# Attention tiles inside the dense blocks: four stages of the second and third tile start one slot later

## The chip, the cores and the metric

One core of a Trainium2 chip runs the whole program. The time is the device time of one execution in microseconds (us). The kernel before takes 1057.63 us in the median of three runs (1057.42 to 1059.7). One more execution was profiled; its rows stand below. TensorE is called PE, its weight loads PEld, VectorE DVE, ScalarE ACT, GpSimd POOL and SyncE SP, as in the profile.

## The reference

The program is three layers one behind the other, all in float32.

```python
# 1. chunked attention: 4 batches, 8 heads, 768 positions, head size 64
for c in range(24):                       # chunks of 32 queries
    k_full = concat([mem_k, k[c*32-16 : c*32+40]])     # 8 memory keys, 16 left, 8 right
    v_full = concat([mem_v, v[c*32-16 : c*32+40]])
    a = softmax(q[c*32 : c*32+32] @ k_full.T / 8)
    out[c*32 : c*32+32] = a @ v_full
x = out as (3072, 512)
# 2. dense layer, 512 -> 2048 -> 512
h = x @ w_in;  x = (h * clip(h + 3, 0, 6) / 6) @ w_out
# 3. eight experts, one for each token, chosen by cosine likeness
logits = normalise(x) @ normalise(expert_emb).T / tau
e = argmax(logits);  gate = softmax(logits)[e]
out = gate * (relu(x @ w1[e]) @ w2[e])
```

## The kernel before

The 3072 tokens are 24 tiles of 128, and the tiles make eight blocks of 4, 2, 3, 3, 3, 3, 3 and 3 (`BS`; `F0` is the first tile of each block). The program goes through the blocks of the dense layer, and while block `bl` is worked on, two other things are laid between its steps: the attention of the three tiles of block `bl + 1`, and the router of block `bl - 1`. Behind the last block comes the expert stage.

A block has 16 steps `f`, one for each 128 of the 2048 inner columns. In a step PE does `mm1(bl, f + 1)` (12 matmuls, L434, into a bank `h`) and later `mm2(bl, f)` (9 matmuls, L488, into three banks `acc`). What is to be laid between stands in dictionaries: `pre_[f]` runs before `mm1(bl, f + 1)`, `slot[f]` between it and `mm2(bl, f)` (L1168 to 1176). A function in a slot issues its instructions on all engines at that place, and every engine works through its own list in this order. ACT and DVE have, behind each `mm1`, the gate of its result: ACT relu (L447), DVE `g` (L448), ACT `gh` (L442), DVE `gl` (L443); `mm2` of the next step needs `gh` and `gl`.

A tile of attention has six stages (`stages(i)`), each in a slot of its own:

- `st_t(i + 1, i)`: keys of the tile after, and queries. From tile 9 on (`VT`, the tenth) DVE transposes the keys (L219) and the queries (L257, tile `qT`), POOL copies the edges of the keys to the neighbouring windows (L223 to 230). Then SP issues the loads of the next keys and queries, 16 small DMAs each (L144).
- `st_s`: 64 small matmuls into the double bank `s` (L275); DVE takes the maximum (L287) and subtracts it (L292, tile `e`), ACT makes exp (L295). In the last tile of a batch DVE sets an edge before that (L285).
- `st_n`: DVE sums and inverts (L308 to 310).
- `st_pt`: four PE transposes of `e` into the bank `att` (L319), ACT copies them out (L321, tile `pT`).
- `st_av`: 64 matmuls into `s` (L333), DVE multiplies (L340, tile `xo`); then SP loads the values of the tile after the next (L178, L188).
- `st_xt`: four PE transposes of `xo` into `att` (L203), ACT makes `xh` (L368), DVE the rest `xl` (L370).

`att` is one PSUM bank. The router uses it too: `r_t` (transposes L525, then a split of four steps in turn on ACT and DVE, L543, L545, L547, L549), `r_l` (12 small matmuls, L558, and a DVE reduction, L561), `r_rank` (L609 to 627) and `r_list` (L649, L650, matmuls with the tiles `sel` that `r_sel` makes on DVE, L639 to 641, three operations for each tile). In blocks with three routed tiles `r_t` stands in slots 1 and 4 and in `pre_[7]`, `r_l` in `pre_[4]`, slot 6 and `pre_[8]`, `r_rank` in slot 9, `r_sel` in slot 10, `r_list` in slot 11, `r_gate` with its three writes to `xb` (SP, L686) in slot 12. The tiles `qT` and `pT` are one buffer, `e` and `xo` another, the bank `s` a third.

The diff touches the numbers that place the stages of blocks 2 to 6. The first tile of a block has slots 0, 1, 2, 3, 4, 5. The second has 4, 5, 6, 7, 9, 10 and the third 9, 10, 11, 12, 14, 15. Stages are put in with `insert(0, ...)`, so in a slot that two tiles share the later tile's stage comes first: in slot 4 `st_t` of the second tile comes ahead of `st_av` of the first, in slot 5 `st_s` of the second ahead of `st_xt` of the first.

Of the kernel before, what the change touches and what calls it, by code (L numbers as in the profile page):

```python
# [30 lines left out]
def attn_moe_kernel(ctx, tc, q, k, v, mem_k, mem_v, w_in, w_out, emb, tau, w1, w2, out, dbg=None):  # L31
# [485 lines left out]
    def r_t(bl, t, pt=None, more=None):  # L517

        if t == 0:
            blk[bl] = (small([P, BS[bl]], name="ss"), small([P, BS[bl], E], name="lg"))  # L520
        x2 = x2_t[bl, t]
        if pt is None:
            pt = bank("att", 1)
        for j in range(KD):
            nc.tensor.transpose(pt[:, j * P:(j + 1) * P], x2[:, j * P:(j + 1) * P], ident)  # L525
        if t == BS[bl] - 1 and more:
            q = [sb.tile([P, DM], BF16, tag=n, name="x2T", bufs=2) for n in ("gh", "gl")]
        else:
            q = sb.tile([P, 2, DM], BF16, tag="dec", name="x2T", bufs=2)
            q = [q[:, i, :] for i in range(2)]  # L530
        mid = late["x2"][2][:, t * DM // 2:(t + 1) * DM // 2] if bl == 0 else x2[:, XW + 1:XW + 1 + DM // 2]
        parts = q[0], mid.bitcast(BF16), q[1]
        x2T[bl, t] = parts
        if more is None:
            split3([(pt, parts)], nc.scalar)
        else:
            more.append((pt, parts))
# [13 lines left out]
    def r_l(bl, t, pl=None):  # L551
        parts = x2T.pop((bl, t))
        own = pl is None
        pl = bank("att", 1) if own else pl[:, 3 * E * t:]
        for j in range(KD):
            for i, xt in enumerate(parts):
                w = (3 - i) * E
                nc.tensor.matmul(pl[:, 0:w], lhsT=xt[:, j * P:(j + 1) * P], rhs=en_t[:, j, 0:3 - i, :].rearrange("p a e -> p (a e)"),  # L558
                                 start=(j == 0 and i == 0), stop=(j == KD - 1 and i == 2))
        if own:  # L560
            V.tensor_reduce(out=blk[bl][1][:, t, :], in_=pl[:, 0:3 * E].rearrange("p (a e) -> p e a", a=3), axis=AX.X, op=ALU.add)  # L561

    def r_ss(bl, t):
        junk = sb.tile([P, DM], F32, tag="dec", name="junk", bufs=2)
        nc.scalar.activation(out=junk, in_=x2_t[bl, t][:, 0:DM], func=AF.Square, accum_out=blk[bl][0][:, t:t + 1])
        if t == BS[bl] - 1:
            blk[bl] = (root(blk[bl][0]),) + blk[bl][1:]
# [16 lines left out]
    def r_route(bl):  # L584

        ss, lg = blk[bl]
        TB = BS[bl]
        sh = [P, TB, E]
        mx = small([P, TB], name="r_mx")
        V.tensor_reduce(out=mx, in_=lg, axis=AX.X, op=ALU.max)  # L590
        eq = small(sh, name="r_eq")
        V.tensor_tensor(out=eq, in0=lg, in1=mx.unsqueeze(2).to_broadcast(sh), op=ALU.is_equal)
        V.tensor_tensor(out=eq, in0=eq, in1=rev.unsqueeze(1).to_broadcast(sh), op=ALU.mult)
        m2 = small([P, TB], name="r_m2")
        V.tensor_reduce(out=m2, in_=eq, axis=AX.X, op=ALU.max)
        oh = small(sh, F16, name="r_oh")
        V.tensor_tensor(out=oh, in0=eq, in1=m2.unsqueeze(2).to_broadcast(sh), op=ALU.is_equal)
        blk[bl] = (ss, lg, oh, mx)
# [46 lines left out]
    def r_list(bl, pT=None, defer=False):  # L645

        pT = (bank("att", 1) if pT is None else pT)[:, 0:NCOL]
        for t, (r0, r1, c) in enumerate(blk[bl][4]):
            nc.tensor.matmul(pT, lhsT=r0, rhs=c, start=(t == 0), stop=False)  # L649
            nc.tensor.matmul(pT, lhsT=r1, rhs=c, start=False, stop=(t == BS[bl] - 1))  # L650

        def add():
            V.tensor_tensor(out=lists, in0=lists, in1=pT, op=ALU.add)

        if defer:
            return add
        add()
# [304 lines left out]
    with tc.manual_schedule():  # L962
# [15 lines left out]
        def stages(i):  # L978
            def a():
                st_t(i + 1 if i + 1 < NT else None, i)  # L980

            def s_():
                st_s(i)

            def p_():
                st_pt(i)

            def v_():
                st_av(i)
                if i + 2 < NT:  # L990
                    load_mv(i + 2)
                    load_v(i + 2)

            def x_():
                st_xt(i)
            return [a, s_, lambda: st_n(i), p_, v_, x_]
# [11 lines left out]
        st = [stages(i) for i in range(BS[0] + BS[1] + 1)]  # L1008
# [95 lines left out]
        def spare(bl):  # L1104

            if bl == NB - 1:
                return bank2()[:, 0, :]
            if bl == 1 and "px" not in late:
                late["px"] = bank("acc", 3)
            return late["px"] if bl == 1 else None  # L1110

        for bl in range(NB):
            slot, pre_ = {}, {}
            if bl == 0:
                continue
            if bl + 1 < NB:
                if bl == 1:
                    slot[0] = [a6[5]]
                for a in range(bl == 1, TB):
                    st = stages(F0[bl + 1] + a)  # L1120
                    for o, f_ in zip((0, 2, 3, 4, 6, 7) if bl == 1 else (0, 1, 2, 3, 4, 5) if a == 0 else (-1, 0, 1, 2, 4, 5), st):
                        slot.setdefault((1, 8)[a - 1] + o if bl == 1 else 5 * a + o, []).insert(0, f_)
            if bl:
                d = 2 if bl == 1 else 0
                for t in range(BS[bl - 1]):
                    (wt, f), (wl, f2) = (RT4 if bl == 1 else RT)[t], (RL4 if bl == 1 else RL)[t]
                    (pre_, slot)[wt].setdefault(f, []).append(lambda t=t: r_t(bl - 1, t, spare(bl)))
                    (pre_, slot)[wl].setdefault(f2, []).insert(0, lambda t=t: r_l(bl - 1, t))
                    slot.setdefault((8, 8, 9, 9)[t] + d // 2, []).append(lambda t=t: r_ss(bl - 1, t))
                slot.setdefault(8 + d, []).append(lambda: r_route(bl - 1))  # L1130
                slot.setdefault(9 + d, []).append(lambda: r_rank(bl - 1))
                slot.setdefault(10 + d, []).append(lambda: r_sel(bl - 1))
                slot.setdefault(11 + d, []).append(lambda: r_list(bl - 1))
                slot.setdefault(12 + d, []).append(lambda: r_exp(bl - 1))
                slot.setdefault(12 + d, []).append(lambda: r_gate(bl - 1))
                if bl == EB + 1:
                    slot.setdefault(12, []).append(pick_first)
                    slot.setdefault(14, []).append(pick_rest)
            if bl == NB - 1:
                at_ctx.close()  # L1140
                p2["pool"] = ctx.enter_context(tc.tile_pool(name="p2", bufs=1, side="right", reuse_waits="tile"))
                for n in range(NE):
                    load_x(("E", n))
                eE = [nc.values_load(e0i[0:1, n:n + 1], engines=[SP], min_val=0, max_val=E - 1) for n in range(2)]
                todo = [(st, p, i) for p in range(4) for st in range(2) for i in range(2)]
                rws = {}

                def pre(n=1):
                    for _ in range(n):
                        if todo:  # L1150
                            st, p, i = todo.pop(0)
                            rws[st, p, i] = load_half(p, i, eE[st])

                def go(st, p, i, eng=None):
                    split_half(st, p, i, rws.pop((st, p, i)), eng)
                    pre()

                pre(RW)
                for n, f in enumerate(SP_):
                    slot.setdefault(f, []).append(lambda n=n: go(n // 2 % 2, n // 4, n % 2, nc.gpsimd if n in PG else None))  # L1160
                slot.setdefault(1, []).append(plan_const)
                slot.setdefault(13, []).append(lambda: T_x(("E", 0)))
            if bl == 1:
                evac(0)
            mm1(bl, 0)
            if bl > 1:
                evac(bl - 1)
            for f in range(KF):  # L1168
                for g_ in pre_.get(f, []):
                    g_()  # L1170
                if f + 1 < KF:
                    mm1(bl, f + 1)
                for g_ in slot.get(f, []):
                    g_()
                if bl < NB - 1 or f < KF - 1:
                    mm2(bl, f)
# [75 lines left out]
        for i in range(2, len(seq)):  # L1252
            n, st = seq[i]
# [70 lines left out]
```

## Time and profile before

| what | value |
|---|---|
| median of three runs | 1057.63 us |
| the profiled execution | 1059.21 us, its span 1057.5 us |
| PE busy | 1006.4 us, 95% of the span |
| DVE, ACT, POOL busy | 529.9, 416.8, 163.6 us |
| blocks 2 to 6 | 218.6 to 630.1 us of the span |
| one of blocks 3 to 6 | 82 us |

The profile counts an engine as idle before an instruction and names what ended the idle time. A step of a block is cut here at the first matmul of `mm1`; such a piece holds `mm1(f + 1)`, slot `f`, `mm2(f)` and `pre_[f + 1]`. Durations are those of the engine's records; neighbouring PE matmuls overlap in them.

### The profile page before, as it was taken

The page shows a single profiled execution, that of the slowest core. Times are in us where ns is not written, and L with a number is a line of the kernel's source. Part 1 is how long each engine was busy: PE and PEld are TensorE (multiplying, and loading weights), DVE is VectorE, ACT ScalarE, POOL GpSimd, SP SyncE. Part 2 cuts the span into 40 slices and gives each one's busy share as a digit, 9 for nine tenths or more (in the row PEclk, how much of TensorE's full clock was granted, in tenths as well). Part 3 has the DMA queues.
Part 4 walks back from the last instruction along what each step waited for, and adds up shares of the span by engine and source line. Part 5 has one row for each costly group of instructions (what it writes and reads, how often), then busy time and mean ns, then how long its engine had stood idle before and what let it go on. Part 6 is the DMA issues. An engine that isn't in the chain of part 4 may idle for free.

```text
span 1057.5 us, 23039 instructions
## 1 busy us (share of the span) xinstructions
PE 1006.4 (95%) x8230; PEld 840.9 (80%) x8230; DVE 529.9 (50%) x1174; ACT 416.8 (39%) x743; POOL 163.6 (15%) x209
## 2 busy tenths in 40 slices
PE   8798999999999999999999999998999999999994
PEld 4576778878888888788888888886888888888783
DVE  5677855544545545545545555755134423326530
ACT  5343444433333333333333334662234523336531
POOL 1133760000000000000000010043112111112210
PEclk9899999999999999999999999999999999999998
DMA  9655531232222222232231122332035514247510
GB/s 193 147 164 174 169 113 37 39 68 32 38 67 31 39 72 31 38 78 32 38 75 29 22 83 103 125 90 71 31 111 157 176 40 148 89 152 241 199 50 22
DMA packets 171837, 95.55 MB, mean 90 GB/s; under 512 B 138709, under 2 KB 146933, under 8 KB 171712
## 3 DMA queue, kind: packets, MB, share of 16 engines
q1 hardware_dynamic: 167104, 80.54, 29.0%
q0 software_dynamic: 4448, 13.42, 4.0%
q8 instruction: 66, 1.08, 0.4%
q14 instruction: 59, 0.48, 0.2%
q10 hardware_dynamic: 160, 0.02, 0.0%
HBM read 156.83 MB, written 13.38 MB: 161 GB/s over the span
## 4 chain that ended last, share of the span: by engine, by line
PE 67%; DVE 12%; issue 7%; ACT 6%; DMA 3%; SPq 2%; POOL 1%; POOLq 0%; DVEq 0%; ACTq 0%
PE acc L488 18%; PE h L434 18%; PE acc L836 11%; PE h L805 11%; PE s L814 2%; PE s L333 1%; DVE g L448 1%; SPq L144 1%; DVE mx L287 1%; ACT g L447 1%; ACT gh L442 1%; DVE e L292 1%; PE att L787 1%; DVE dec L412 1%; PE att L319 1%
## 5 line engine op out<-in xcount | busy, mean ns | idle before, releaser
L488 PE MATMUL acc<-wo,gh 128*128 128x512 f32 x640 | 206.5, 404 | 2.5 <-DVE x L505 1.5
L434 PE MATMUL h<-xh,w_in_h 128*128 128x384 f32 (+2 forms) x512 | 175.7, 343 | 5.6 <-DVE wo L470 2.4
L434 PE MATMUL h<-xl,w_in_h 128*128 128x384 f32 (+2 forms) x512 | 173.1, 338 | 0.1
L434 PE MATMUL h<-xh,w_in_l 128*128 128x384 f32 (+2 forms) x512 | 172.5, 337 | 0.0
L447 ACT ACTIVATE g<-h,three 128x384 f32<-128x384 f32 (+1 forms) x112 | 63.4, 566 | 176.9 <-PE h L434 176.2
L488 PEld LDWEIGHTS acc<-wo,gh 128*128 128x128 f32 x640 | 113.1, 188 | 23.0 <-ACT x L507 2.6
L488 PE MATMUL acc<-wo,gl 128*128 128x512 f32 x320 | 126.2, 394 | 0.0
L448 DVE SCALAR_TENSOR_TENSOR g<-g,h 128x384 f32<-128x384 f32 (+1 forms) x112 | 59.8, 534 | 127.3 <-ACT g L447 126.7
L434 PEld LDWEIGHTS h<-xh,w_in_h 128*128 128x128 f32 x512 | 96.4, 188 | 14.4 <-DVE wo L470 3.9
L434 PEld LDWEIGHTS h<-xl,w_in_h 128*128 128x128 f32 x512 | 96.6, 189 | 7.2 <-DVE xl L370 1.0
L434 PEld LDWEIGHTS h<-xh,w_in_l 128*128 128x128 f32 x512 | 96.4, 188 | 2.9
L443 DVE TENSOR_TENSOR gl<-g,gh 128x384 fp32r<-128x384 f32 (+1 forms) x112 | 60.8, 543 | 63.2 <-ACT gh L442 63.2
L442 ACT CAST gh<-g 128x384 fp32r<-128x384 f32 (+1 forms) x112 | 55.8, 498 | 77.7 <-DVE g L448 77.7
L792 DVE TENSOR_TENSOR tl<-att,th 128x512 fp32r<-128x512 f32 x26 | 18.0, 692 | 113.5 <-ACT th L791 107.6
L488 PEld LDWEIGHTS acc<-wo,gl 128*128 128x128 f32 x320 | 60.1, 188 | 14.2 <-DVE gl L443 0.6
L773 POOL DMA_INDIRECT xg<-xb,m_ix x27 | 27.9, 1032 | 261.9 <-PE h L805 212.2
L223 POOL COPY kt<-kt 128x192 f32<-128x192 f32 x15 | 5.2, 346 | 373.5 <-DVE kt L219 373.5
L836 PE MATMUL acc<-wo,th 128*128 128x512 f32 x192 | 60.6, 397 | 0.0
L791 ACT CAST th<-att 128x512 fp32r<-128x512 f32 x26 | 15.2, 587 | 107.3 <-PE acc L836 105.6
L808 ACT ACTIVATE hs<-h 128x512 f32<-128x512 f32 x54 | 32.1, 597 | 64.3 <-PE h L805 60.4
L836 PE MATMUL acc<-w_in_h,th 128*128 128x512 f32 x120 | 49.0, 408 | 0.0
L805 PE MATMUL h<-wo,th 128*128 128x512 f32 x192 | 48.9, 397 | 0.0
(318 smaller groups left out, 1820.0 us busy)
## 6 DMA issues: line engine op xcount, KB each, us to landing
rw<-in_moe_w_dram SPq DMA_DIRECT2D x136, 512.0 KB
vw<-in_v_dram SPq DMA_DIRECT2D x176, 56.0 KB
raw_in<-in_moe_w_in_dram SPq DMA_DIRECT2D x16, 512.0 KB
raw_out<-in_moe_w_out_dram SPq DMA_DIRECT2D x16, 512.0 KB
xb<-x SPq DMA_DIRECT2D x20, 256.5 KB
k_t<-in_k_dram SPq DMA_DIRECT2D x240, 16.0 KB
q_t<-in_q_dram SPq DMA_DIRECT2D x240, 16.0 KB
k_t<-in_k_dram SPq DMA_DIRECT2D x9, 256.0 KB
```

The costliest lines, as they stand in the source:

```text
L434: nc.tensor.matmul(hp, lhsT=wt[:, c, f * P:(f + 1) * P], rhs=xc, start=(n == 0), stop=(n == 3 * KD - 1))
L442: nc.scalar.copy(out=gh, in_=g)
L443: nc.vector.tensor_tensor(out=gl, in0=g, in1=gh.bitcast(F32), op=ALU.subtract)
L447: nc.scalar.activation(out=g, in_=hp, func=AF.Relu, bias=three)
L448: nc.vector.scalar_tensor_tensor(out=g, in0=g, scalar=6.0, in1=hp, op0=ALU.min, op1=ALU.mult)
L488: nc.tensor.matmul(acc[bl][t], lhsT=gt[:, t * P:(t + 1) * P], rhs=wo[hl, f // 2][:, f % 2, :], start=(f == first and n == 0), stop=(f == l ...
L773: nc.gpsimd.indirect_dma_start(out=t[:, :], out_offset=None, in_=src, in_offset=bass.IndirectOffsetOnAxis(ap=ix[:, 0:1], axis=0), bounds_c ...
L792: V.tensor_tensor(out=tl[:, 0:KD, :], in0=x3, in1=th[:, 0:KD, :].bitcast(F32), op=ALU.subtract)
L805: nc.tensor.matmul(hp, lhsT=a[:, kk, :], rhs=wpart(st, hl, p, kk), start=(kk == 0 and a is th and hl == 0), stop=(kk == KD - 1 and a is tl))
L808: nc.scalar.activation(out=h_t[n][:, p, :], in_=hp_t.pop((n, p)), func=AF.Relu)
L814: nc.tensor.transpose(hp[:, j * P:(j + 1) * P], h[:, j * P:(j + 1) * P], ident)
L836: nc.tensor.matmul(o, lhsT=a[:, KD + f, :], rhs=wpart(st, hl, 2 + half, kk), start=(f == 0 and c == 0), stop=(f == KE - 1 and c == 2))
```

## The change

The stages `st_t`, `st_s`, `st_n` and `st_pt` of the second and third tile of blocks 2 to 6 get slots 5, 6, 7, 8 and 10, 11, 12, 13. `st_av` and `st_xt` keep theirs. The first tiles, block 1 and the router keep their slots. Each engine gets the same instructions in another order.

```diff
                 for a in range(bl == 1, TB):
                     st = stages(F0[bl + 1] + a)
-                    for o, f_ in zip((0, 2, 3, 4, 6, 7) if bl == 1 else (0, 1, 2, 3, 4, 5) if a == 0 else (-1, 0, 1, 2, 4, 5), st):
+                    for o, f_ in zip((0, 2, 3, 4, 6, 7) if bl == 1 else (0, 1, 2, 3, 4, 5), st):
                         slot.setdefault((1, 8)[a - 1] + o if bl == 1 else 5 * a + o, []).insert(0, f_)
```

Slots 4 to 13 before and after, in PE's order (2nd and 3rd are tiles; `mm1` and `mm2` left out; what stands on no PE list in brackets):

```
slot   before                           after
4      [2nd t] 1st av, r_t              1st av, r_t
5      2nd s, 1st xt                    [2nd t] 1st xt
6      r_l [2nd n]                      r_l, 2nd s
7      r_t, 2nd pt                      r_t [2nd n]
8      r_l [r_ss, r_route]              r_l, 2nd pt [r_ss, r_route]
9      [3rd t] 2nd av, r_rank           2nd av, r_rank
10     3rd s, 2nd xt [r_sel]            [3rd t] 2nd xt [r_sel]
11     r_list [3rd n]                   3rd s, r_list
12     3rd pt [r_exp, r_gate]           [3rd n, r_exp, r_gate]
13                                      3rd pt
```

(`r_t` of slot 7 and `r_l` of slot 8 stand in `pre_`, in front of the `mm1` of that step.)

## Rows read from the trace of the kernel before

**Rows 1.** The page, part 1: busy us, share of the span, instructions.

```profile
PE 1006.4 (95%) x8230; PEld 840.9 (80%) x8230; DVE 529.9 (50%) x1174; ACT 416.8 (39%) x743; POOL 163.6 (15%) x209
```

**Rows 2.** Windows: length, busy us of PE, PEld, DVE, ACT, POOL, clock, DMA, GB/s.

```profile
695.00:1057.00 362.00, 344.33 (x1711) 284.62 (x1709) 135.99 (x242) 147.01 (x205) 71.00 (x58) 0.98 0.34 110
```

**Rows 3.** PE's waits, blocks 2 to 6: us in total, times, longest.

```profile
PE att L649 <- DVE sel L640: 3.1, 5, 0.7
PE att L319 <- DVE x2T L549: 3.0, 4, 0.8
PE acc L488 <- DVE x L505: 1.5, 1, 1.5
PE att L203 <- DVE x2T L549: 1.3, 2, 1.1
...
PE att L558 <- DVE xl L370: 0.7, 3, 0.2
```

**Rows 4.** Windows, columns as in rows 2: a piece without stages, block 5, slot 2.

```profile
478.31:482.45 4.14, 4.14 (x22) 3.77 (x21) 2.29 (x4) 2.17 (x4) 0.00 (x0) 1.00 0.20 31
```

**Rows 5.** Timeline of DVE, block 5: start, us, engine, line, operation, tiles, shapes, count.

```profile
491.96 0.70 DVE L219 STREAM_TRANSPOSE kt<-k_t 128x512 f32<-128x512 f32 x1
492.59 0.67 DVE L257 STREAM_TRANSPOSE qT<-q_t 128x512 f32<-128x512 f32 x1
...
497.08 0.56 DVE L443 TENSOR_TENSOR gl<-g,gh 128x384 fp32r<-128x384 f32 x1 [0.58 <-ACT gh L442]
...
500.21 0.69 DVE L370 TENSOR_TENSOR xl<-att,xh 128x512 fp32r<-128x512 f32 x1 [1.17 <-ACT xh L368]
...
503.22 0.68 DVE L308 TENSOR_REDUCE sm<-e 128x8 f32<-128x512 f32 x1
...
506.11 0.69 DVE L549 TENSOR_TENSOR x2T<-att,x 128x512 bf16<-128x512 f32 x1 [0.65 <-ACT x L547]
...
508.05 0.56 DVE L443 TENSOR_TENSOR gl<-g,gh 128x384 fp32r<-128x384 f32 x1 [0.58 <-ACT gh L442]
...
526.59 0.69 DVE L370 TENSOR_TENSOR xl<-att,xh 128x512 fp32r<-128x512 f32 x1 [1.17 <-ACT xh L368]
...
528.67 0.32 DVE L641 TENSOR_SCALAR sel<-io,r_part,pid 128x128 f16<-128x128 f16 x1
```

**Rows 6.** Timeline of PE, block 1: list matmuls whose `sel` tiles were ready.

```profile
209.87 0.26 PE L649 MATMUL att<-sel 128*128 128x192 f16 x1
209.96 0.25 PE L650 MATMUL att<-sel 128*128 128x192 f16 x1
```

**Rows 7.** Windows of PE, sums over blocks: slots 11, 7, 3, 6, 5; one slot 5.

```profile
sum 31.72, PE 27.89; mean PE 5.58
...
sum 23.74, PE 20.75; mean PE 5.19
...
sum 19.67, PE 19.67; mean PE 4.92
...
sum 21.22, PE 20.44; mean PE 5.11
...
492.99:498.53 5.54, 5.54 (x91) 1.00 0.21 32
...
sum 29.46, PE 27.82; mean PE 5.56
```

**Rows 8.** Timeline of PE, block 5, slot 7: idle time before it in brackets.

```profile
506.95 0.63 PE L319 MATMUL att<-ident,e 128*128 128x128 f32 x4 [0.75 <-DVE x2T L549]
```

**Rows 9.** Timeline of POOL, block 5: the last copy behind L219.

```profile
493.47 0.21 POOL L230 COPY kt<-kt 128x32 f32<-128x32 f32 x1
```

**Rows 10.** Timelines of SP and DVE, block 2; SP, block 5; ACT, block 6.

```profile
237.63 7.66 SPq L144 DMA_DIRECT2D q_t<-in_q_dram  x16
...
248.81 0.71 DVE L257 STREAM_TRANSPOSE qT<-q_t 128x512 f32<-128x512 f32 x1 [1.48 <-DMA k_t<-in_k_dram]
...
538.91 1.31 SPq L686 DMA_DIRECT2D xb<-x  x3
...
551.77 1.08 ACT L507 ACTIVATE x<-acc 128x512 f32<-128x512 f32 x2
```

The sums of rows 7 go over these pieces: slot 11 of blocks 2 to 6 (five), slot 7 of blocks 3 to 6 (four), slot 3 of blocks 3 to 6 (four: `st_pt` of the first tile and `r_l`), slot 6 of blocks 3 to 6 (four), slot 5 of blocks 2 to 6 (five).

## The prediction

> **What bounds the kernel now.** I read the page's busy shares first: TensorE (PE) is busy for 95% of the span [rows 1], so only time in which PE waits, or starts late, can be won. Next the table by stretches: the expert stage behind the last dense block has 362 us with 344.33 us of PE work [rows 2]; nothing in it is touched, it is only started earlier or later. The change touches blocks 2 to 6, so I asked there for PE's waits [rows 3]. Four of them lie in steps whose place is moved or next to one: the list matmuls (L649, slot 11) wait for VectorE's (DVE's) `sel` tiles; `st_pt` of the second tile (L319, slot 7) waits for the router split (L549); `st_xt` of the first tile (L203, slot 5) waits for such a split too, mostly in block 2; the router's small matmuls (L558, slot 6) wait for `xl` of that `st_xt`. Last come pieces of one slot each, cut at the first matmul of `mm1`. A piece with `mm1`, `mm2` and nothing else takes 4.14 us [rows 4], the floor against which the others are held. The reader should see that PE is never slow there, its granted clock is 1.00 in all these pieces; it is late because one PSUM bank, "att", goes in turn through the router, `st_pt` and `st_xt`, and each user waits for VectorE and ScalarE (ACT) to empty it.
>
> **The change part by part.** Ten tiles (second and third of blocks 2 to 6) have `st_t`, `st_s`, `st_n`, `st_pt` one slot later; `st_av` and `st_xt` stay. No instruction is added or removed; what counts is what each queue has in front of what PE waits for.
>
> *Slot 11, the list matmuls (rows "L649").* Before, VectorE has behind `gl` of slot 10: max, subtract, then a pause until ACT has done exp and `xh`, then `xl`. In slot 5, which has the same order, `gl` ends at 497.08 + 0.56 = 497.64 and `xl` at 500.21 + 0.69 = 500.90, so 3.26 us later [rows 5]. Afterwards two transposes stand there, which follow each other at 0.63 us (491.96 to 492.59) [rows 5]; `xh` no longer queues behind exp, and `xl` comes at once: 3 x 0.63 = 1.89 us. So `sel` starts 1.37 us sooner, and its nine operations still end 528.98 - 527.28 = 1.70 us after `xl` [rows 5]. PE gets to the list matmuls at the same moment as before, as the scores move from in front of `mm2` to in front of them. Unhindered they follow each other at 0.09 us [rows 6], so six of them cost 0.5. The five pieces took 31.72 us [rows 7]. Afterwards I expect 4.14 + 0.5 + 0.2 (about 0.1 for the last `sel`, still just behind, and 0.1 for the change of shape) = 4.85 in four of them, 4.6 in block 2, which routes two tiles only: 24.0, without the scores. Gain 7.7 us. The bound from below is what the wait rows alone give, 3.1 [rows 3].
>
> *Slot 7, `st_pt` of the second tile.* It goes to slot 8, and what remains in slot 7 is not PE's. The pieces of blocks 3 to 6 with the wait sum to 23.74 us, four with the same contents and no wait to 19.67 [rows 7]: 4.07, less 0.08 each for the start behind the split's transposes, 3.75 us. What is late next: in slot 8 `st_pt` needs the bank from the third router tile, whose reduction stands on VectorE behind L549, `g` and `gl` (508.05 + 0.56 - 506.80 = 1.81 us behind the end of L549) and `st_n` (about 1.0, of which 0.68 is its reduction) [rows 5], so about 3.0 us behind L549. L549 itself ended at 506.80; now max, subtract and exp stand in front of the split instead of `st_n` (2.1 of the 2.57 us between `gl` and the start of `xl`, against 1.0), and all of it starts 0.85 us sooner, by what PE needs for the scores (slot 5 took 5.54, so 1.40 over the floor, for `st_s` with `st_xt` [rows 4, 7]; about 0.55 of that stays): 507.05, the bank is free at 510.05. PE was at `st_pt` in slot 7 at 506.95 - 0.75 = 506.2 [rows 8]; a piece later (4.92 less 0.45 for the transposes themselves) and 0.4 ahead it gets there at 510.3. It should not wait, by 0.2 us.
>
> *Slot 6, the router matmuls.* `xl` is ready 1.37 us sooner, PE arrives some 0.85 us sooner since the scores have left slot 5. Blocks 3 to 6 sum to 21.22 [rows 7]; without the wait I hold them to the 4.92 of a piece with as many transposes and router matmuls (19.67 / 4), so 1.5, and 0.2 for block 2: 1.7 us. The margin is about 0.2 us. The scores behind them need POOL's copies, whose last ends 1.02 us after the key transpose (493.47 + 0.21 against 491.96 + 0.70) [rows 5, 9]: before `xl` ends, so hidden.
>
> *Slot 5, `st_xt` of the first tile.* The two transposes (1.26 us, as above) no longer stand in slot 4 in front of `xo` and the split L549, which so ends 1.26 us sooner, against 0.85 us by which PE asks sooner. In block 2 a DMA wait of 1.48 us for the queries stood in front as well [rows 10]. The five pieces sum to 29.46; undisturbed one takes 5.54 [rows 7]: 29.46 - 27.70 = 1.76 us.
>
> *Loads.* SP issues 32 loads of keys and queries behind each `st_t`, about 16 us of its queue: in block 2 the last 16 start at 237.63, take 7.66, and the transpose could start at 248.81, so they landed about 3.5 us after the last issue [rows 10]. With slots 0, 5, 10 the distances are 5, 5 and 6 slots of over 4.9 us instead of 4, 5 and 7, so each has at least 5 x 4.9 = 24 us for 20: the shortest distance, which had the wait, becomes longer. The value loads of `st_av` now go in front of those loads, as SP's order follows the slots. In slot 12 the three writes to `xb` (issued from 538.91 to 540.22 before [rows 10]) come behind the third tile's loads: its key transpose ends 0.63 behind `gl` (526.59 - 2.57 + 0.63 = 524.65 [rows 5]), the loads take 16, the writes 1.3, so the last is issued at 541.9, less 1.4 for what the block has won by then. They must land before the next block evacuates `acc` (L507, at 551.77 [rows 10], less a whole block's gain of 3). I cost all of this at nothing: the writes would have some 8 us, and the loads above landed in 3.5.
>
> *Sum.* 7.7 + 3.75 + 1.7 + 1.76 = 14.9 us. Two of the checks (slots 6 and 8) come out within 0.2 us of a wait, in five blocks and in four; I charge 0.1 us for each of the nine: 14.0. The profiled execution took 1059.21 us (span 1057.5) and would take 1045.2; it is 1.6 above the median 1057.63, from which I forecast 1043.6.
>
> A rule to hold against this: the Trainium skill ("SBUF — State Buffer", section "SBUF: two separate sides") says that VectorE and GpSimd have one pair of ports in common, taken as a lock by a VectorE operation in a two-port mode or with two SBUF inputs, so that the other stands still. `xl` has one input in PSUM, so by that text nothing would stand still; the query transpose beside which the copies lie now takes 0.67 us [rows 5, 9], the one in block 2 that waited until they were over 0.71 [rows 10], so no stop is seen there. By the lock the forecast would be that of the second rival below.
>
> **The rivals.**
> 1. *The waits go, the restarts don't.* Then only what the rows call a wait comes back: 3.1 + 3.0 + 1.3 + 0.7 = 8.1 us [rows 3]: 1049.5. Against it: the undisturbed pieces, 4.92 and 5.54 us, are measured and lie below by more than the wait [rows 7]. Chance 0.18.
> 2. *VectorE's new order delays `xl`.* If POOL's copies, 0.9 us [rows 5, 9], held up `xl`, the margin of 0.2 in slot 6 would become a wait of 0.7 in five blocks (3.5) and `sel` would be 0.9 late in four (3.6): a gain of 14.0 - 7.1 = 6.9, 1050.7. Against it: the query transpose beside them is no longer for it [rows 5, 10]; `xl` itself was not beside them. Chance 0.10.
> 3. *No change: given back later.* The expert stage could wait for its weights instead. It has 362 - 344 = 18 us without PE work [rows 2]. But its first loads are issued at the last block's start, and move with it. 1057.6, chance 0.05.
> 4. *Slower: the `xb` writes.* They are issued behind 32 loads in slot 12; the tiles that they free are the ones into which the next block evacuates `acc`, and `mm2` of its slot 0 waits for that. They have 8 us; each further microsecond would cost PE one in each of five blocks. From 8 + 14 / 5 = 10.8 us after issue on it eats the whole gain. At 12 us it would be 5 x 4 = 20 us against 14: 1063.6. For it: in block 2 PE already waits 1.5 us for that evacuation (L505) [rows 3]. Against it: the landing of about 3.5 us. Chance 0.04.
>
> **How the numbers follow.** Forecast 0.63 (gains of 11 to 17 us: 1040.6 to 1046.6), rivals 0.18, 0.10, 0.05, 0.04. 0.2%, some 2 us, is what a measurement here can tell from no change. Faster 0.63 + 0.18 + 0.10 = 0.91, same 0.05, slower 0.04. The range takes in rival 1 and the nearer half of rival 2: 1041 to 1050. Its lower end is the whole 14.9 with 1.7 for list matmuls and bank changes even less hindered than I took them.
>
> **What would show it.** The waits L649, L319 and L558 gone from PE's list or under 0.2 us each; pieces of slot 11 at 4.9 plus the scores; the end of `xl` 1.9 us behind that of `gl`; no wait for a DMA at the key and query transposes, nor for L507 or L505 beyond the present 0.2 us. Wrong it would be if `st_pt` in slot 8 waited for the reduction L561 by more than 0.3 us, if `xl` stretched beside POOL's copies, or if the last block started sooner and the end didn't.

## The result, and the profile after

The changed kernel takes 1045.65 us in the median (1044.95 to 1046.91, four runs) against 1057.63 (four runs); the ratio is 0.9884, 95% interval 0.9867 to 0.9901. A second measurement on another chip gave 1044.32 against 1060.0, ratio 0.9868 (0.9846 to 0.9890). So 12 to 16 us are gained; 1043.6 was forecast. The profiled execution took 1045.22 us, its span is 1043.5. Of 32 later executions of the kernel before, the nine in which PE's mean granted clock was 0.991 and more took 1055.9 to 1057.7 us, the other 23, at 0.983 to 0.990, took 1058.6 to 1064.6.

Windows of the kernel before and then of the changed one, cut at the start of block 2 and of block 7 (length, busy us of PE, PEld, DVE, ACT, POOL, clock, DMA share, GB/s):

```profile
0.00:218.64 218.64, 197.68 (x2121) 153.24 (x2122) 144.12 (x320) 95.51 (x207) 67.20 (x79) 0.98 0.50 127
218.64:630.06 411.42, 399.64 (x4025) 345.02 (x4024) 211.84 (x529) 140.45 (x275) 16.93 (x62) 1.00 0.23 46
630.06:1057.50 427.44, 409.06 (x2087) 342.68 (x2085) 173.94 (x327) 180.82 (x261) 79.50 (x68) 0.99 0.35 115
```

```profile
0.00:220.60 220.60, 198.12 (x2121) 153.78 (x2122) 144.18 (x320) 95.53 (x207) 67.22 (x79) 0.97 0.50 126
220.60:616.49 395.89, 393.15 (x4025) 345.81 (x4024) 209.49 (x529) 139.87 (x275) 17.08 (x62) 1.00 0.24 47
616.49:1043.50 427.01, 409.65 (x2087) 343.29 (x2085) 173.80 (x327) 180.68 (x261) 80.32 (x68) 0.98 0.35 115
```

Blocks 2 to 6 are 411.42 - 395.89 = 15.53 us shorter. The time ahead of them, in which the code is the same, was 1.96 us longer in this one execution: PE's first scores (L275) started at 12.56 us instead of 10.44, behind a wait of 1.83 us for a DMA (L975; 0.43 before) and a granted clock of 0.50 to 0.55 from 8.70 to 12.21 us (1.00 before). The time behind blocks 2 to 6 is the same to 0.4 us.

PE's idle time in these blocks fell from 11.8 to 2.7 us, by 9.0. The other 6.5 us are busy time, although the 4025 PE matmuls are the same. Of these, 4.4 us lie in slots 10 to 13. There the six list matmuls were fed one by one before, 0.23 to 0.34 us from start to start, which counts as busy all the same (block 5, slot 11 of the kernel before):

```profile
527.68 0.26 PE L649 MATMUL att<-sel 128*128 128x192 f16 x1 [0.43 <-DVE sel L640]
527.91 0.26 PE L650 MATMUL att<-sel 128*128 128x192 f16 x1
528.25 0.24 PE L649 MATMUL att<-sel 128*128 128x192 f16 x1
...
529.04 0.26 PE L650 MATMUL att<-sel 128*128 128x192 f16 x1
```

The other 2.1 us of busy time lie in slots 5 to 8, where the other waits were.

PE's waits of the changed kernel in blocks 2 to 6 (in total, times, longest), to be held against [rows 3]:

```profile
PE acc L488 <- DVE x L505: 1.8, 1, 1.8
PE acc L488 <- ACT x L507: 0.8, 4, 0.2
```

L649, L319, L203 and L558 are gone. (The lists of waits under the experiments reach some us into block 7; where L507 stands with five waits, the fifth is there.) DVE in slots 5 to 8 and 10 of block 5, as in [rows 5]:

```profile
489.76 0.56 DVE L443 TENSOR_TENSOR gl<-g,gh 128x384 fp32r<-128x384 f32 x1 [0.58 <-ACT gh L442]
490.24 0.70 DVE L219 STREAM_TRANSPOSE kt<-k_t 128x512 f32<-128x512 f32 x1
490.87 0.67 DVE L257 STREAM_TRANSPOSE qT<-q_t 128x512 f32<-128x512 f32 x1
491.46 0.65 DVE L370 TENSOR_TENSOR xl<-att,xh 128x512 fp32r<-128x512 f32 x1
...
498.79 0.69 DVE L549 TENSOR_TENSOR x2T<-att,x 128x512 bf16<-128x512 f32 x1 [0.65 <-ACT x L547]
...
502.04 0.13 DVE L561 TENSOR_REDUCE lg<-att 128x8 f32<-128x24 f32 x1
...
516.45 0.65 DVE L370 TENSOR_TENSOR xl<-att,xh 128x512 fp32r<-128x512 f32 x1
...
518.49 0.31 DVE L641 TENSOR_SCALAR sel<-io,r_part,pid 128x128 f16<-128x128 f16 x1
```

From the end of `gl`, 490.32, to that of `xl`, 492.11, are 1.79 us now, 3.26 before. PE in the same block: the router matmuls of slot 6, `st_pt` in slot 8, the list matmuls of slot 11, to be held against [rows 6, 8]:

```profile
492.35 0.19 PE L558 MATMUL att<-en_t,x2T 128*128 128x24 bf16 x1
...
502.79 0.60 PE L319 MATMUL att<-ident,e 128*128 128x128 f32 x4
```

```profile
518.28 0.26 PE L649 MATMUL att<-sel 128*128 128x192 f16 x1
518.37 0.25 PE L650 MATMUL att<-sel 128*128 128x192 f16 x1
518.45 0.25 PE L649 MATMUL att<-sel 128*128 128x192 f16 x1
518.54 0.25 PE L650 MATMUL att<-sel 128*128 128x192 f16 x1
518.62 0.24 PE L649 MATMUL att<-sel 128*128 128x192 f16 x1
518.85 0.26 PE L650 MATMUL att<-sel 128*128 128x192 f16 x1
```

The first five start 0.08 to 0.09 us apart; only the last stands 0.23 behind, as its `sel` ends at 518.80. The router matmuls start 0.24 us behind `xl`, `st_pt` 0.62 behind the reduction L561. In sums over pieces of blocks 2 to 6, the piece starts read from PE's timeline, slots 5 to 8 went from 105.0 to 97.4 us, slots 10 to 13 from 103.3 to 95.1, all others together lost 0.2.

### The profile page after: what moved, and what is told of

The parts are those of the page before. It is cut to its first block, busy times and chain, and to the rows that moved or that the text cites. A ratio compares the mean times of both kernels' runs of the same rounds, so it can differ in the third digit from the quotient of the medians.

```text
span 1043.5 us, 23013 instructions
## 1 busy us (share of the span) xinstructions
PE 1000.9 (96%) x8230; PEld 842.9 (81%) x8230; DVE 527.5 (51%) x1174; ACT 416.1 (40%) x743; POOL 164.6 (16%) x209
## 4 chain that ended last, share of the span: by engine, by line
PE 79%; DVE 7%; issue 5%; ACT 3%; DMA 2%; POOL 1%; SPq 1%; POOLq 0%; DVEq 0%; ACTq 0%
PE h L434 22%; PE acc L488 21%; PE acc L836 12%; PE h L805 12%; PE s L814 2%; PE s L333 1%; PE s L275 1%; PE att L787 1%; DVE dec L412 1%; PE att L319 1%; DMA out_dram<-r,m_tid 1%; PE att L203 1%; PE att L525 1%; PE att L558 1%; SPq L178 1%
```

## The experiments

Six kernels and one repetition tell the terms apart, and one joins what they point to. The first four shared a chip (before: 1059.75), the other four a second one (before: 1060.0).

**Third tile alone**

```diff
-... (0, 1, 2, 3, 4, 5) if a == 0 else (-1, 0, 1, 2, 4, 5), st):
+... (0, 1, 2, 3, 4, 5) if a != 1 else (-1, 0, 1, 2, 4, 5), st):
```

> Only the third tile of blocks 2 to 6 has its four stages one slot later; the second keeps the early slots. Theory (each wait is worked off where the stage stands): the list wait L649 goes (3.1 us of waits before), waits L319 (3.0), L558 (0.7) and L203 (1.3) stay; blocks 2 to 6 take 411.4 - 7.8 = 403.6 us, the whole 1057.6 - 7.8 = 1049.8. Rival (the loads: what helped is the longer distance from the first tile's loads to the second's transposes): nothing is gained, 1057.6, and the DMA wait of 1.5 us at the query transpose in block 2 stays with L649 as long as before.

1052.66 us, ratio 0.9935 (0.9914 to 0.9955); blocks 2 to 6 take 403.83 us, a gain of 7.6. PE's waits there:

```profile
PE att L319 <- DVE x2T L549: 3.0, 4, 0.8
PE acc L488 <- DVE x L505: 1.8, 1, 1.8
PE acc L488 <- ACT x L507: 0.9, 5, 0.2
PE att L558 <- DVE xl L370: 0.7, 3, 0.2
PE att L203 <- DVE x2T L549: 0.4, 2, 0.2
```

As the theory has it, L649 is the wait that goes. One number missed: L203 came to 0.4 us, not 1.3, and slot 5 took 1.3 us less than before. The wait for the queries in block 2, which stood ahead of it, was 0.2 us in this execution instead of 1.5, without any change to these loads: part of that term is chance of the execution. Another chance took more back: slots 0 and 1 of block 2 were 1.7 us longer than before, as PE waited 0.3 us longer for L505 and its granted clock stood at 0.50 right behind that wait (0.81 over slot 1). Slots 10 to 13, the ones that this edit moves, gave 8.0 us; that the sum over the blocks came so near to 7.8 is in part luck.

**Second tile alone**

```diff
-... (0, 1, 2, 3, 4, 5) if a == 0 else (-1, 0, 1, 2, 4, 5), st):
+... (0, 1, 2, 3, 4, 5) if a < 2 else (-1, 0, 1, 2, 4, 5), st):
```

> Only the second tile is moved. Theory: L319, L558, L203 go, L649 stays at 3.1 us; blocks 2 to 6 take 411.4 - 7.7 = 403.7 us, the whole 1049.9; with the run that moves the third alone the two gains add up to the whole 15.5 us that blocks 2 to 6 gave. Rival (the loads): the whole gain, 395.9 us in blocks 2 to 6 and 1045.6.

1051.77 us, ratio 0.9927 (0.9896 to 0.9958); blocks 2 to 6 take 403.92 us, a gain of 7.5. PE's waits:

```profile
PE att L649 <- DVE sel L640: 3.4, 5, 0.8
PE acc L488 <- DVE x L505: 1.5, 1, 1.5
PE acc L488 <- ACT x L507: 1.0, 5, 0.2
```

The two gains add up to 15.1 of 15.5 us; in the slots that each moves, 7.5 (slots 5 to 8) and 8.0 (slots 10 to 13), they make the 15.5. The rival of the loads falls: this kernel has the longer way from the first tile's loads to the second's transposes, and gets only its own half.

**`st_pt` alone**

```diff
-... (-1, 0, 1, 2, 4, 5), st):
+... (-1, 0, 1, 3, 4, 5), st):
```

> Of the second and third tile only st_pt goes one slot later. Theory: the wait L319 goes with its restart, 3.75 us, 4.1 at the most (four pieces from 5.94 to 4.92 and less); L649, L558, L203 stay; blocks 2 to 6 take 407.6 us, the whole 1053.9. Rival (only the idle time in the rows comes back, not the restart): 3.0 us, 408.4 and 1054.6. Rival (the router split is late by itself and holds st_pt in slot 8 as well): no gain, 1057.6.

1057.37 us, ratio 0.9971 (0.9953 to 0.9989); blocks 2 to 6 take 409.08 us, 2.3 us gained where 3.75 were expected. PE's waits:

```profile
PE att L649 <- DVE sel L640: 3.4, 5, 0.8
PE acc L488 <- DVE x L505: 2.6, 1, 2.6
PE att L203 <- DVE x2T L549: 1.8, 3, 1.1
PE acc L488 <- ACT x L507: 0.8, 4, 0.2
PE att L558 <- DVE xl L370: 0.4, 2, 0.2
```

Piece by piece the theory holds: slots 7 and 8 together went from 49.52 to 45.85 us, 3.67 less, more than the 3.0 of idle time, so the restart (what a wait costs PE beyond its idle time) comes back with the wait. What took 1.1 us from it lies at block 2's slot 0, before any stage that was moved: L505 waited 2.6 us for DMA writes, against 1.5 in the profile before; the rest is in slot 5 (29.85 against 29.46).

**`st_t` stays early**

```diff
-... (-1, 0, 1, 2, 4, 5), st):
+... (-1, 1, 2, 3, 4, 5), st):
```

> st_s, st_n and st_pt go one slot later, st_t (transposes and loads) keeps its early slot. Theory (what stands ahead on VectorE counts): L649, L319 and L558 go, xl comes 0.7 us behind gl; but the two transposes stay in slot 4 ahead of the split L549 while PE asks for the bank 0.85 us sooner, so st_xt (L203) in slot 5 waits some 0.7 us in blocks 3 to 6 and over 1.9 in block 2 with the DMA wait still there: 15.5 - 1.8 - 3.5 = 10.2 us gained, 401.2 in blocks 2 to 6, the whole 1047.4. Rival (the place of the transposes does not matter, only that of the scores): 395.9 and 1045.6.

1050.58 us, ratio 0.9911 (0.9882 to 0.9940); blocks 2 to 6 take 400.45 us, a gain of 11.0 where 10.2 were expected. PE's waits:

```profile
PE att L203 <- DVE x2T L549: 4.4, 5, 1.3
PE acc L488 <- DVE x L505: 1.5, 1, 1.5
PE acc L488 <- ACT x L507: 1.1, 5, 0.2
```

The place of the transposes is worth 4.6 us: left in slot 4 they hold the split L549, and `st_xt` in slot 5, which asks sooner now, waits in every block. Its slots 5 sum to 28.36 us against 22.95 in the changed kernel. The wait for the queries in block 2, expected there with over 1.9 us, did not come: its slot 5 took 5.49 us, as in most other blocks. The list is even better off, 27.77 against 28.24 us in slot 11, with `xl` 0.62 us behind `gl`.

**The changed kernel again**

> The changed kernel once more, for its gain on this chip and as the measure for the others of this call. Theory: blocks 2 to 6 take 395.9 us within 0.5 us whatever the execution, against 411.4; what differs between executions by a microsecond or two lies ahead of block 2 and in its first piece (the wait of L505 for the DMA of block 0's writes). So the whole is 15.5 us below the kernel before, less up to 2. Rival (something behind block 6 gives time back): the stretch from block 7 on is longer than the 427.0 and 427.4 us of the two profiles by 1 us and more.

1044.32 us, ratio 0.9868 (0.9846 to 0.9890). Blocks 2 to 6 take 396.59 us in its profile, 0.7 more than in the first where 0.5 was allowed; 0.4 of it is block 2. The stretch behind is 427.6. Nothing is given back. Over the profiles of these kernels block 2 starts at 217.6 to 220.6 us though all but three have the same code up to there: the 2 us between the forecast and the median are of that size.

**Edges on VectorE**

```diff
-        eng = nc.gpsimd if i >= VT else nc.vector
+        eng = nc.vector
```

> The changed kernel with the copies of the key edges made by VectorE instead of POOL, so between key and query transposes, ahead of xl. POOL takes 0.9 us for the four; VectorE's price is not in the trace, 0.4 to 1.1 us. Theory (VectorE's list ahead of xl is the next limit, with no margin left in slots 6 and 11): PE waits that long again in slot 6 of five blocks (L558 on xl) and in slot 11 of four (L649 on sel), 9 x 0.4 to 1.1 = 4 to 10 us slower than the changed kernel, the two waits back in the list. Rival (there is a margin of half a microsecond): under 2 us slower. Rival (POOL's copies beside VectorE were what held it, a lock on ports in common): not slower.

1051.69 us, 7.4 more than the changed kernel beside it; blocks 2 to 6 take 403.25, 6.7 more. DVE in slot 5 of block 5, then PE's waits:

```profile
493.53 0.70 DVE L219 STREAM_TRANSPOSE kt<-k_t 128x512 f32<-128x512 f32 x1
494.27 0.26 DVE L223 COPY kt<-kt 128x192 f32<-128x192 f32 x1
...
494.67 0.18 DVE L230 COPY kt<-kt 128x32 f32<-128x32 f32 x1
494.75 0.71 DVE L257 STREAM_TRANSPOSE qT<-q_t 128x512 f32<-128x512 f32 x1
495.38 0.65 DVE L370 TENSOR_TENSOR xl<-att,xh 128x512 fp32r<-128x512 f32 x1
```

```profile
PE acc L488 <- DVE x L505: 2.3, 1, 2.3
PE att L558 <- DVE xl L370: 1.1, 5, 0.3
PE acc L488 <- ACT x L507: 1.0, 5, 0.2
PE s L275 <- DVE qT L257: 0.8, 4, 0.2
```

The copies put 1.22 - 0.63 = 0.59 us between the transposes. Slots 6 rose by 1.7 and slots 11 by 2.4 us, so VectorE's list is the next limit there. In slot 6 of blocks 3 to 6 `xl` came 0.53 to 0.63 us later behind `gl` and PE lost 0.32 to 0.42: 0.2 us were hidden, the margin that the prediction had. In slot 11 of blocks 3 to 5 `xl` came 0.55 to 0.89 us later and all of it came through. The rival of ports in common falls, as the kernel is slower. A third place I had not named is slot 1, 2.3 us in all. In blocks 3 to 6 it took 0.9, as the first tile's scores wait for the query transpose. The other 1.4 us are in block 2 and are none of the copies': behind the wait for L505 PE's granted clock stood at 0.50, its lower level (1.2 GHz), here from 228.20 to 231.50 us (length, busy us of PE, clock, DMA share, GB/s):

```profile
228.20:231.50 3.30, 3.30 (x12) 0.50 0.10 15
```

Without this the edit costs blocks 2 to 6 some 5.3 us, within the 4 to 10 expected.

**Writes of block 0 sooner**

```diff
-                slot.setdefault(12 + d, []).append(lambda: r_exp(bl - 1))
-                slot.setdefault(12 + d, []).append(lambda: r_gate(bl - 1))
+                slot.setdefault(12, []).append(lambda: r_exp(bl - 1))
+                slot.setdefault(12, []).append(lambda: r_gate(bl - 1))
```

> The changed kernel with r_exp and r_gate of block 0 (run in block 1) in slot 12 instead of 14, so its writes to xb go to SP some 8 us sooner, ahead of the value loads of the last tile. Theory (the one wait left at the start of block 2, 1.8 us of PE on L505, is the landing of these writes, about 4.4 us from issue): the wait goes, block 2 takes 78.3 us instead of 80.2, the whole 1.9 us less than the changed kernel on this chip. Rival (the buffer is freed by something else, or VectorE's extra work in slot 12 delays sel or the list there): no gain, or PE waits in block 1 longer by as much.

1042.69 us against 1044.32 beside it; to the kernel before 0.9836 (0.9818 to 0.9853). Block 2 takes 77.61 us, 2.6 less than in the first profile of the changed kernel and 3.0 less than in the second, and one wait is left in blocks 2 to 6:

```profile
PE acc L488 <- ACT x L507: 1.0, 5, 0.2
```

PE's waits in block 1 are the same, to 0.1 us for each. The gain in the block is larger than the wait: slot 0 alone went from 6.40 to 4.28 us, 2.1 less, with 1.8 us of idle time. Of the whole program the times do not show this gain: the medians differ by 1.6 us and the two intervals overlap. The stretch behind block 6 took 428.4 us in this profile, against 427.0 and 427.6; whether the edit has a part in that is not shown.

**Both**

```diff
-... (0, 1, 2, 3, 4, 5), st):
+... (0, 1, 2, 3, 4, 5) if a < 2 else (-1, 1, 2, 3, 4, 5), st):
```

(with the edit of the run before)

> As the one before, and the third tile's st_t goes back to slot 9 (its scores and the rest stay late). Theory: slot 11 has no wait for sel left at all, as xl comes right behind gl: 0.15 us less in each of blocks 3 to 5, 0.5 us in all, as in the run that kept st_t early; the split L549 does not stand behind the third tile's transposes, so slot 9 costs nothing. 1.9 + 0.5 = 2.4 us below the changed kernel. Rival (the transposes ahead of xo in slot 9 delay st_xt in slot 10): slower than the run before by 0.3 us and more.

1041.4 us (1038.93 to 1041.72), ratio to the kernel before 0.9818 (0.9799 to 0.9837), whose interval lies wholly below that of the changed kernel on the same chip, 0.9846 to 0.9890. It beats the kernel before and the changed one; the kernel with the sooner writes alone it betters by 0.5 us in blocks 2 to 6 of the profile, as expected, while their intervals overlap.

```profile
218.72:611.67 392.95, 392.11 (x4024) 345.88 (x4023) 209.77 (x529) 139.90 (x275) 16.95 (x62) 1.00 0.25 46
```

PE is busy for 392.11 of the 392.95 us of blocks 2 to 6; slot 11 is at 27.77, as where `st_t` stayed early, and slot 10 at 23.11, so the third tile's early transposes cost nothing.

## Why the prediction was right

- *Slot 11* was the largest term, 7.7 us. Slots 10 to 13 gave 8.2, and 8.0 with the third tile alone. `xl` comes 1.79 us behind `gl` where 1.89 was worked out (slots 5 and 10 of block 5), and the last `sel` is still the one that PE waits for, as foreseen.
- *Slot 7, slot 6 and slot 5* were 3.75, 1.7 and 1.76, together 7.2 us. Slots 5 to 8 gave 7.6, the second tile alone 7.5, and `st_pt` alone 3.67 in its slots. That a wait costs its restart too, the difference between 8.1 us of idle time [rows 3] and 14.9, was the step on which the number hung; rival 1 would have been 1049.5. The profile has it as 9.0 us of idle and 6.5 us of busy time.
- *The charge of 0.9 us* for tight margins was not needed: `st_pt` in slot 8 stands 0.6 us behind the reduction, not 0.2, and nothing waits there. In slot 6 the margin of 0.2 us held: the router matmuls start 0.24 us behind `xl`. The whole came to 15.5, nearer to the 14.9 without it.
- *Loads and writes* at nothing: right. No wait for a DMA at the transposes is left, and the evacuation L507 of blocks 3 to 7 waits 0.2 us as before. The "present 0.2 us" of the prediction holds for L507 alone: L505 in block 2 took 1.5 us already [rows 3] and takes 1.8 now. SP issued the three writes of block 5's slot 12 from 531.94; ACT empties `acc` at 541.57:

```profile
531.94 1.36 SPq L686 DMA_DIRECT2D xb<-x  x3
```

  Those are 8 us, as estimated.
- *Rival 2* (POOL's copies hold `xl`): POOL's copies lie from 491.08 to 491.96 now, and `xl`, beside them from 491.46 on, took 0.65 us. With the copies on DVE, and POOL idle beside it, `xl` took 0.65 as well: they don't stretch it. Moving them off POOL made the kernel slower.
- *From profile to median*: the forecast took 14.0 us off a median. The profiles show 15.5 in the blocks, the medians 12.0 on one chip and 15.7 on the other. The prediction said nothing of this spread of executions; its range of 1041 to 1050 covered it. Part of it lies ahead of block 2, where the two profiles differ by 1.96 us. The four executions behind 1057.63 may have been quick ones, as the kernel before took 1059.75 and 1060.0 in the medians of 21 and 11; this stays open. The 14.0 lies between the two medians and 1.5 us below what the blocks gave.

## What to carry to other kernels

When stages of several tiles are laid between the steps of one engine, look at what stands in front of each awaited result in the list of the engine that makes it: here two operations that wait on no other engine in front of `xl`, in place of a chain through two engines, were worth 1.5 us each time. Price a wait of PE by comparing whole pieces with and without it: the piece with 0.75 us of idle time was 1.02 us longer than its undisturbed like, and the list with its six matmuls fed one by one cost about 1.6 us more (8.2 us in five blocks) than with five of them ready, of which 0.6 is in the list of waits.

## What the runs showed of the hardware that was not expected

DMA landings differ between executions of the same code: at the start of block 2 DVE waited 2.0 to 3.1 us for the same writes to `xb` (L505), and the wait for the queries in block 2 was 1.5, 1.2 or 0.2 us in three kernels with the same loads ahead of it. The four edge copies take 0.9 us on POOL; on DVE they put 0.6 us between two transposes.

PE's granted clock fell to 0.50 in block 2 of two kernels, behind idle times of 1.8 and 2.3 us at L505, and the next `mm1` matmuls started 0.32 us apart instead of 0.17; that cost slots 0 and 1 some 1.4 us each time. In two others the same wait, 2.2 and 2.6 us long, was followed by a clock of 1.00. What decides between the two is not shown, and so a difference of this size between two profiles need not come from an edit.
